# Two pairs of heads taken by turns at the end of an attention stage, and a routing step asked for earlier

## The chip, the cores and the metric

The kernel runs on one core of one Trainium2 chip. The metric is device microseconds of one execution; less is better. Shown times are medians of several runs of the same program. The engines are TensorE (PE in the rows, PEld for its weight loads), VectorE (DVE), ScalarE (ACT), GpSimd (POOL) and SyncE (SP, which here only issues DMAs). Each works through its own list of instructions in the order in which they stand there, and waits at an instruction until what it needs is there.

## The reference, cut to what matters

Three stages in float32, on 2 batches of 8 heads, 768 positions, head size 64:

```python
# 1. attention: a band of |i - j| < 16, and blocks of 32 keys (max of k, mean of v)
scores_l = where(|pos_i - pos_j| < 16, q @ k.T / 8, -1e9)
scores_s = q @ k.reshape(B, H, 24, 32, D).max(3).T / 8 + log(32)
a = softmax(concat([scores_l, scores_s]));  out = a @ concat([v, v_blockmean])
# 2. experts: x [1536, 512]; logits = x @ w_gate; all (token, expert) pairs in falling order of
#    logit, each token to its first expert that holds under 192 tokens so far
out[mask_e] = relu(x[mask_e] @ w1[e]) @ w2[e]          # 8 experts, 192 tokens each
# 3. h = x @ w_in; s = h * softmax(h); layer norm of s times g_ln; out = ln @ w_out
```

## The kernel before, in words

**The units.** The attention runs in 24 units. A unit is (batch, pair of heads, group), where a group is four of the twelve blocks of 64 queries. The list `units` (line 322) numbers them: batch by batch, pair by pair, group by group. A unit passes through three steps: `score` (line 325; four products on PE, L331, then on DVE the mask and the row's extreme, L337, then four exponentials on ACT, L340), `attnT` (L347 turns the weights on PE, L349 empties PSUM on ACT into `aT`) and `pv` (L360 multiplies with the values on PE; DVE makes a reciprocal, L363 and L364, and writes the scaled result into `x`, L367).

**What feeds a pair.** `prep` readies a pair's keys and queries in three steps: GpSimd or DVE copy the keys (L275 `kr`), PE turns keys (L291) and queries (L299) into the PSUM tile `T`, of which there are two, DVE (L293) or ACT (L302) empty it into `kTw` and `qbd`.

**What a group gives.** When all four pairs of a batch are done for a group, its 256 tokens are whole. Then `pv` stores them to HBM (L371), `xT` turns each block of 128 tokens on PE (L381) and empties it on ACT (even blocks, L386) or DVE (odd blocks, L384), and `logits` multiplies by the gate (L393); DVE copies the result into `L` (L395). Batch 1 has blocks 6 to 11, two for each group. `pA` (two in PSUM) serves `attnT` and `xT`, `pO` (two) serves `pv` and `logits`.

**What follows.** The routing of the first expert begins with `head` (line 125): some twelve short DVE instructions over blocks of `L`. It is called twice for the first expert: for blocks 0 to 7 inside the attention (line 450), for blocks 8 to 11 by `route(0)` after it. Only then does `route(0)` go on: a search in five rounds of DVE and PE, the expert's index, its weights' DMA, its products. The whole second half of the kernel hangs on this.

**What sets the order.** A table `plan` gives each step a due time counted in units; the steps are written in rising order of it. For a step of a unit `u`: `score` at u, `attnT` at u + 1.9, `pv` at u + 3.3 (for the last three), `prep` of a pair at the index of its first unit less 4.5, 3.5 and 2.5, `xT` at the index of the last pair's unit + 4.6 and + 5.3, `logits` 1.1 later. PE and SP keep the order in which the steps are written. DVE, ACT and POOL are ordered by a scheduler from its own estimates. Three chunks of the third stage's weights (`raw`, 512 KB each) are also split in this stretch, in six instructions each: L70 and L77 on ACT, L72, L74, L75 and L78 on DVE.

Of the kernel before, what the change touches and what calls it, by code (L numbers as in the profile page):

```python
# [21 lines left out]
def tile_attention_moe_solu(ctx, tc, q, k, v, w_gate, w1, w2, w_in, w_out, g_ln, out):  # L22
    nc = tc.nc
    B, H, S, D = q.shape
# [4 lines left out]
    HP = H // 2  # L29
# [132 lines left out]
    r0 = ctx.enter_context(tc.tile_pool(name="r0", bufs=1))  # L162
    SPLIT = NJ * 2 // 3
    T0 = {}
# [155 lines left out]
            e.tensor_copy(a[:, :NT - 1, 80:WIN], a[:, 1:, 16:32])  # L320

    units = [(b, hp, g) for b in range(B) for hp in range(HP) for g in range(3)]
    ST, AT, XS = {}, {}, {}

    def score(u):
# [74 lines left out]
    def at(u, f, *a):  # L400
        plan.setdefault(u, []).append((f, a))

    for u in range(NU):
        b, hp, g = units[u]
# [42 lines left out]
    with tc.manual_schedule(engines={mybir.EngineType.PE, mybir.EngineType.SP}):  # L447
        for n in range(3):
            prep(0, 0, n)
        at(27.71, head, r0, T0, 0, SPLIT)  # L450
        for u in sorted(plan):
            for f, a in plan[u]:
                f(*a)
# [514 lines left out]
```

## Time and profile before

| | us |
|---|---|
| runs shown (3): median, lowest, highest | 483.68, 482.17, 484.4 |
| profiled execution, its own time | 481.84 |
| its span in the trace | 480.1 |
| PE busy | 444.0 (92%) |
| DVE busy | 273.8 (57%) |
| ACT busy | 175.1 (36%) |

The span is what the trace covers; the run's own time is 1.74 us longer. The last PE instruction of the attention ends at 100.9 us of the span, and the second part of `head` begins at 101.21. Up to there PE, DVE and ACT work on different units side by side, and which of them is late changes from stretch to stretch. From there to about 125 us PE mostly waits for short DVE instructions, one after another; then PE is busy nearly without a break to the end.

### The profile page before, as it was taken

To read this page: it belongs to the slowest core of one execution; us is meant where nothing else is said; L and a number is where in the kernel's file an instruction comes from. 1 tells how busy PE (TensorE), PEld (TensorE's weight loads), DVE (VectorE), ACT (ScalarE), POOL (GpSimd) and SP (SyncE) were. 2 spreads that over 40 slices of the span, in tenths; PEclk is the share of its full clock that TensorE was granted. 3 is DMA by queue.
4 is the path that set the end of the run, shared out by engine and by line. 5 is a ranking of instruction groups with operands and counts; after the bars stand their busy time and mean duration, and the time that the engine had idled before them with its cause. 6 is when DMAs were issued, how large, how long until landed. Compare 5 with 4: busy or idle time off the path is not lost.

```text
span 480.1 us, 9909 instructions
## 1 busy us (share of the span) xinstructions
PE 444.0 (92%) x3809; PEld 385.4 (80%) x3809; DVE 273.8 (57%) x1049; ACT 175.1 (36%) x425; POOL 58.9 (12%) x120
## 2 busy tenths in 40 slices
PE   2899999856989999999999999999999999999994
PEld 1668688735888998788888888888898899998773
DVE  8668576977596879960756249153742404132441
ACT  3678877700243336411313213231131314222331
POOL 8221200001010020020001100201102000101001
PEclk9999999977999999999999999999999999999998
DMA  9969961273889487066019102900752740000001
GB/s 205 219 147 208 231 170 58 89 255 125 271 251 308 122 303 224 2 200 206 1 40 339 50 1 88 319 0 4 248 155 81 224 124 1 23 1 12 11 23 44
DMA packets 92463, 64.62 MB, mean 135 GB/s; under 512 B 25728, under 2 KB 87168, under 8 KB 92416
## 3 DMA queue, kind: packets, MB, share of 16 engines
q1 hardware_dynamic: 88848, 51.93, 39.2%
q0 software_dynamic: 1984, 6.29, 3.7%
q10 hardware_dynamic: 1584, 5.77, 3.5%
q8 instruction: 30, 0.49, 0.4%
q14 instruction: 17, 0.14, 0.1%
HBM read 56.51 MB, written 6.29 MB: 131 GB/s over the span
## 4 chain that ended last, share of the span: by engine, by line
PE 74%; DVE 13%; ACT 4%; DMA 4%; issue 3%; POOL 1%; POOLq 0%; SPq 0%; ACTq 0%; DVEq 0%
PE m L695 30%; PE h L760 13%; PE o L803 11%; PE pS L331 4%; PE pO L360 2%; DVE ge L123 2%; PE pr L501 2%; PE pA L347 2%; PE tr L667 1%; DVE ex L769 1%; PE T L291 1%; PE T L254 1%; PE T L299 1%; DMA kn<-in_k_dram 1%; DVE ch L74 1%
## 5 line engine op out<-in xcount | busy, mean ns | idle before, releaser
L695 PE MATMUL m<-xs,wr 128*128 128x192 f32 x384 | 77.4, 333 | 0.2 <-ACT xs L673 0.2
L695 PEld LDWEIGHTS m<-xs,wr 128*128 128x128 f32 x384 | 63.2, 190 | 4.7 <-PE o L803 0.8
L743 DVE TENSOR_TENSOR yl<-m,yh 128x128 fp32r<-128x128 f32 (+1 forms) x64 | 16.2, 253 | 73.4 <-ACT yh L742 72.7
L712 ACT ACTIVATE hT<-m 128x192 f32<-128x192 f32 x64 | 21.2, 332 | 90.6 <-PE m L695 77.1
L695 PE MATMUL m<-hT,wh 128*128 128x192 f32 x256 | 49.9, 327 | 0.0
L695 PE MATMUL m<-hT,wl 128*128 128x192 f32 x256 | 49.2, 327 | 0.0
L695 PEld LDWEIGHTS m<-hT,wl 128*128 128x128 f32 x256 | 43.3, 189 | 3.2
L695 PEld LDWEIGHTS m<-hT,wh 128*128 128x128 f32 x256 | 43.3, 189 | 3.2
L742 ACT CAST yh<-m 128x128 fp32r<-128x128 f32 (+1 forms) x64 | 15.2, 238 | 82.8 <-PE m L695 73.9
L340 ACT ACTIVATE s<-s,mx 128x120 f32<-128x120 f32 x96 | 31.4, 387 | 11.9 <-DVE mx L337 11.8
L760 PE MATMUL h<-wiH,yh 128*128 128x512 f32 x96 | 34.5, 447 | 0.0
L803 PE MATMUL o<-woH,lh 128*128 128x512 f32 x96 | 30.8, 433 | 1.3 <-ACT lh L792 1.3
L760 PE MATMUL h<-wiH,yl 128*128 128x512 f32 x96 | 32.0, 421 | 0.0
L803 PE MATMUL o<-woL,lh 128*128 128x512 f32 x96 | 31.9, 429 | 0.0
L760 PE MATMUL h<-wiL,yh 128*128 128x512 f32 x96 | 31.8, 419 | 0.0
L331 PE MATMUL pS<-kTw,qbd 128*128 128x120 f32 x192 | 27.3, 287 | 4.6 <-DVE kTw L314 3.6
L331 PEld LDWEIGHTS pS<-kTw,qbd 128*128 128x128 f32 x192 | 24.4, 199 | 6.4 <-issue 4.8
L765 DVE TENSOR_REDUCE st<-h 128x1 f32<-128x1024 f32 x12 | 14.7, 1224 | 26.0 <-PE h L760 25.5
L123 DVE TENSOR_TENSOR ge<-e,ios 128x1536 bf16<-128x1536 bf16 (+3 forms) x37 | 29.0, 783 | 0.8
L803 PE MATMUL o<-woH,ll 128*128 128x512 f32 x96 | 29.3, 417 | 0.0
L337 DVE CUSTOM_DVE_ANT_0 s<-pS,mask 128x120 f32<-128x120 f32 x96 | 21.4, 278 | 12.0 <-PE pA L347 5.2
L501 PEld LDWEIGHTS <-ge 128*128 128x128 bf16 (+1 forms) x420 | 13.8, 96 | 15.2 <-DVE ge L123 10.2
(184 smaller groups left out, 797.7 us busy)
## 6 DMA issues: line engine op xcount, KB each, us to landing
wr<-in_moe_w_dram SPq DMA_DIRECT2D x24, 512.0 KB
wl<-in_moe_w_dram SPq DMA_DIRECT2D x20, 512.0 KB
wh<-in_moe_w_dram SPq DMA_DIRECT2D x20, 512.0 KB
raw<-in_moe_w_out_dram ACTq DMA_DIRECT2D x8, 512.0 KB
Vw<-in_v_dram SPq DMA_DIRECT2D x20, 192.0 KB
kn<-in_k_dram SPq DMA_DIRECT2D x8, 384.0 KB
qn<-in_q_dram SPq DMA_DIRECT2D x8, 384.0 KB
xd<-x SPq DMA_DIRECT2D x6, 512.0 KB
```

The lines of the kernel that those rows point to most:

```text
L123: nc.vector.tensor_tensor(out, x.rearrange("p (j t) -> p j t", t=2)[:, :, None, :].to_broadcast([128, n // 2, b - a, 2]), ios[:, None, a:b ...
L331: nc.tensor.matmul(p[:, n, :], qbd[i][:, t, :], kTw[i][:, t, :], start=True, stop=True)
L337: nc.vector.tensor_tensor_reduce(s[:, n, :], p[:, n, :], m, scale=1.0, scalar=3.0e38, op0=OP.add, op1=OP.min, accum_out=mx[:, n:n + 1])
L340: EXPS[u] = nc.scalar.activation(s[:, n, :], s[:, n, :], AF.Exp, bias=mx[:, n:n + 1], scale=-1.0)
L501: nc.tensor.matmul(pr[0:nb, 0:E], ge[:, j // 2, :nb, j % 2], oh[:, j, :], start=j == 0, stop=j == NJ - 1)
L695: nc.tensor.matmul(p[:, :CAP], w[:, d, o:o + 128], rhs[:, d], start=d == 0, stop=d == n - 1)
L712: after(ph, "h", f, nc.scalar.activation(h[:, f], p[:, :CAP], AF.Relu))
L742: a = nc.scalar.copy(hi, s[:, s0:s0 + n])
L743: nc.vector.tensor_tensor(YL[k][:, d, c:c + n], s[:, s0:s0 + n], hi.bitcast(F32), op=OP.subtract)
L760: nc.tensor.matmul(ps, a[:, d, :], w[:, d, 512 * s:512 * s + 512], start=n == 0, stop=n == len(mm) - 1)
L765: nc.vector.tensor_reduce(st[:, 0:1], p, axis=AX.X, op=OP.max)
L803: nc.tensor.matmul(p, a[:, f, :], w[:, f, :], start=n == 0, stop=n == len(mm) - 1)
```

## The change

```diff
     units = [(b, hp, g) for b in range(B) for hp in range(HP) for g in range(3)]
+
+    units[-6:] = [(B - 1, hp, g) for g in range(3) for hp in (HP - 2, HP - 1)]
     ST, AT, XS = {}, {}, {}
...
         for n in range(3):
             prep(0, 0, n)
-        at(27.71, head, r0, T0, 0, SPLIT)
+        at(26.1, head, r0, T0, 0, SPLIT)
```

The last six units were (1,2,0) (1,2,1) (1,2,2) (1,3,0) (1,3,1) (1,3,2); now they are (1,2,0) (1,3,0) (1,2,1) (1,3,1) (1,2,2) (1,3,2). So unit 19 completes group 0 (before: unit 21), unit 21 completes group 1 (before: 22), unit 23 still completes group 2. All due times that are taken from a unit's index move: `prep` of pair (1,3) by two units (14.5, 15.5, 16.5 in place of 16.5, 17.5, 18.5), `xT` and `logits` of blocks 6 and 7 by two, of blocks 8 and 9 by one. The first part of `head` is due at 26.1 in place of 27.71. No instruction is added or taken away. SP and POOL have the same rows in the same order in both kernels, and from the second part of `head` on so have PE, DVE and ACT. In the changed kernel every line after 322 has a number greater by 2.

**PE where pair (1,3) is prepared.** Before, from the `pv` behind the score of unit 14 on (`T<-..kr` are keys, `T<-..qn` queries, `kTw_142` belongs to units 15 to 17):

```order
L360 MATMUL pO<-Vw,aT 64x65 x8
L291 MATMUL T<-ident,kr 128x128 x2
L299 MATMUL T<-ident,qn 128x128 x3
L331 MATMUL pS<-kTw_142,qbd_143 128x120 x4
L381 MATMUL pA<-ident,x 128x128 x4
L347 MATMUL pA<-ident,s 120x128 x4
L360 MATMUL pO<-Vw,aT 64x65 x8
L299 MATMUL T<-ident,qn 128x128 x3
L381 MATMUL pA<-ident,x 128x128 x4
```

And the same place in the changed kernel:

```order
L362 MATMUL pO<-Vw,aT 64x65 x8
L291 MATMUL T<-ident,kr 128x128 x2
L299 MATMUL T<-ident,qn 128x128 x3
L291 MATMUL T<-ident,kr 128x128 x4
L333 MATMUL pS<-kTw_142,qbd_143 128x120 x4
L383 MATMUL pA<-ident,x 128x128 x4
L349 MATMUL pA<-ident,s 120x128 x4
L362 MATMUL pO<-Vw,aT 64x65 x8
L299 MATMUL T<-ident,qn 128x128 x3
L291 MATMUL T<-ident,kr 128x128 x2
L299 MATMUL T<-ident,qn 128x128 x3
L383 MATMUL pA<-ident,x 128x128 x4
```

The four key transposes of pair (1,3) now stand directly behind two other fillings of `T`, ahead of the score of unit 15, and in the next unit three fillings of `T` stand in a row.

**PE at the end of the attention.** Before, from the score of unit 23 on (`pA<-ident,s` is `attnT`, `pA<-ident,x` is `xT`, `pO<-wg,xT` is `logits`):

```order
L331 MATMUL pS<-kTw_136,qbd_137 128x120 x4
L360 MATMUL pO<-Vw,aT 64x65 x8
L347 MATMUL pA<-ident,s 120x128 x4
L360 MATMUL pO<-Vw,aT 64x65 x8
L347 MATMUL pA<-ident,s 120x128 x4
L360 MATMUL pO<-Vw,aT 64x65 x8
L381 MATMUL pA<-ident,x 128x128 x4
L360 MATMUL pO<-Vw,aT 64x65 x8
L381 MATMUL pA<-ident,x 128x128 x8
L393 MATMUL pO<-wg,xT 32x8 x16
```

And in the changed kernel, from the `pv` behind the score of unit 23 on:

```order
L362 MATMUL pO<-Vw,aT 64x65 x8
L383 MATMUL pA<-ident,x 128x128 x4
L349 MATMUL pA<-ident,s 120x128 x4
L362 MATMUL pO<-Vw,aT 64x65 x8
L383 MATMUL pA<-ident,x 128x128 x4
L395 MATMUL pO<-wg,xT 32x8 x16
L349 MATMUL pA<-ident,s 120x128 x4
L362 MATMUL pO<-Vw,aT 64x65 x8
L395 MATMUL pO<-wg,xT 32x8 x16
L383 MATMUL pA<-ident,x 128x128 x4
L362 MATMUL pO<-Vw,aT 64x65 x8
L383 MATMUL pA<-ident,x 128x128 x4
```

`xT` of block 6 moved ahead of `attnT` of unit 22, and before the last `pv` (unit 23) there now stand three `xT` and two `logits` in place of one `xT`. Behind the last row shown come, in the changed kernel, the logits of blocks 8 and 9, then `xT` of blocks 10 and 11 together, then their logits.

**ACT at the end of the attention.** Before, behind the copy of `aT` of unit 21 (`cy` and `wiH` belong to the split of the weights' chunks):

```order
L77 CAST wiH<-ch 128x512
L340 ACTIVATE s<-s,mx 128x120 x2
L349 COPY aT<-pA 120x512
L340 ACTIVATE s<-s,mx 128x120 x2
L77 CAST wiH<-ch 128x512
L70 ACTIVATE cy<-raw 128x512
L349 COPY aT<-pA 120x512
L386 COPY xT<-pA 128x512
```

And in the changed kernel:

```order
L77 CAST wiH<-ch 128x512
L342 ACTIVATE s<-s,mx 128x120 x4
L77 CAST wiH<-ch 128x512
L70 ACTIVATE cy<-raw 128x512
L388 COPY xT<-pA 128x512
L351 COPY aT<-pA 120x512 x2
```

The copy of `aT` of unit 22 stood between the exponentials of unit 23, ahead of the third chunk's `cy`; now it stands behind that `cy` and behind the copy of `xT` of block 6.

## Rows read from the trace of the kernel before

**Rows 1.** The page's line of busy time by engine.
```profile
PE 444.0 (92%) x3809; PEld 385.4 (80%) x3809; DVE 273.8 (57%) x1049; ACT 175.1 (36%) x425; POOL 58.9 (12%) x120
```

**Rows 2.** Busy time by stretch: PE, PEld, DVE, ACT, POOL; then clock, DMA, GB/s.
```profile
60.00:88.00 28.00, 28.00 (x495) 24.71 (x493) 21.83 (x118) 22.56 (x60) 2.08 (x6) 1.00 0.33 99
88.00:94.00 6.00, 4.02 (x62) 3.06 (x60) 5.92 (x25) 4.21 (x10) 0.00 (x0) 1.00 0.27 87
94.00:100.00 6.00, 5.37 (x197) 4.39 (x196) 5.47 (x23) 2.27 (x4) 0.00 (x0) 1.00 0.72 262
101.00:102.00 1.00, 0.34 (x8) 0.24 (x7) 0.90 (x9) 0.00 (x0) 0.00 (x0) 0.55 0.07 16
```

**Rows 3.** Timeline, last `pv` to second part of `head`: start, length, engine, line, operation.
```profile
94.04 0.73 PE L360 MATMUL pO<-Vw,aT 120*64 120x65 f32 x16
...
94.71 1.09 PE L381 MATMUL pA<-ident,x 128*128 128x128 f32 x8
94.81 0.16 DVE L363 TENSOR_SCALAR r<-pO 128x4 f32<-128x4 f32 x1
...
96.01 0.41 DVE L367 TENSOR_TENSOR x<-pO,r 128x256 f32<-128x256 f32 x1
...
98.05 0.22 DVE L137 TENSOR_REDUCE v<-L 128x8 f32<-128x64 f32 x1
...
99.16 0.69 DVE L384 COPY xT<-pA 128x512 f32<-128x512 f32 x1
99.77 0.16 DVE L395 COPY L<-pO 128x8 f32<-128x8 f32 x1
...
100.21 0.21 DVE L123 TENSOR_TENSOR ge<-e,ios 128x128 bf16<-128x128 bf16 x1
...
100.50 0.42 PE L393 MATMUL pO<-wg,xT 128*32 128x8 f32 x27 [0.20 <-issue]
...
100.97 0.17 DVE L395 COPY L<-pO 128x8 f32<-128x8 f32 x1 [0.55 <-PE pO L393]
...
101.21 0.18 DVE L137 TENSOR_REDUCE v<-L 128x4 f32<-128x32 f32 x1
```

**Rows 4.** The chain that ended last, 84 to 103 us: start, length, what.
```profile
96.45 4.77 DMA xd<-x
```

**Rows 5.** Timeline, units 13 to 15.
```profile
57.42 0.96 POOL L275 COPY kr<-kn 128x384 f32<-128x384 f32 x2 [1.74 <-DMA kn<-in_k_dram]
...
61.58 0.49 PE L299 MATMUL T<-ident,qn 128*128 128x128 f32 x3
61.78 0.42 DVE L293 COPY kTw<-T 128x256 f32<-128x256 f32 x1
61.91 1.05 PE L331 MATMUL pS<-kTw,qbd 128*128 128x120 f32 x8
...
63.77 0.73 PE L360 MATMUL pO<-Vw,aT 120*64 120x65 f32 x16
...
64.95 0.42 DVE L367 TENSOR_TENSOR x<-pO,r 128x256 f32<-128x256 f32 x1
```

**Rows 6.** Timeline behind the score of unit 23.
```profile
88.06 0.73 PE L360 MATMUL pO<-Vw,aT 120*64 120x65 f32 x16
...
89.41 0.59 ACT L349 COPY aT<-pA 120x512 f32<-120x512 f32 x1
...
89.96 0.41 DVE L367 TENSOR_TENSOR x<-pO,r 128x256 f32<-128x256 f32 x1
...
90.89 0.17 DVE L364 RECIPROCAL r<-r 128x4 f32<-128x4 f32 x1
...
91.51 0.69 ACT L70 ACTIVATE cy<-raw 128x512 f32<-128x512 f32 x1 [0.43 <-DMA raw<-in_moe_w_in_dram]
```

**Rows 7.** The instructions on tile `qn`: ns least, median, most; first and last start.
```profile
L299 PE MATMUL T<-ident,qn x42: 272/273/330, 16.7 to 77.3; 128*128 128x128 f32 x42
...
L299 PE MATMUL pA<-ident,qn x6: 421/421/421, 7.7 to 8.8; 128*128 128x128 f32 x6
```

## The prediction

> **What bounds the kernel now.** I read the page's busy times first: PE is busy for 444.0 of 480.1 us [rows 1]. That is an average, so the table of busy time by stretch comes next, for the stretch that the change touches. From 60 to 88 us PE is busy for all of 28.00 us: there PE is the bound, and what makes it wait is lost. From 88 to 94 it drops to 4.02 of 6 while DVE has 5.92, and from 94 to 100 DVE still has 5.47 of 6 [rows 2]: the end of the attention belongs to DVE. Then I read the timeline up to the second part of `head`, at 101.21 [rows 3]. Everything later hangs on that instruction, and none of its order changes, so the forecast is one question: how far does 101.21 move? The chain of waits names a store of `x`, 4.77 us from 96.45, as the last thing before it [rows 4]. I don't follow it there: `head` reads `L`, not that store, and DVE ran up to 101.14 on a copy that PE's logits released (100.97 + 0.17) [rows 3].
>
> **The middle: `prep` of pair (1,3), two units earlier.** PE's list now has five fillings of `T` within two units where three stood, and `T` has two buffers.
>
> *First wait.* The key transposes of (1,3) follow three query transposes, which begin at 61.58 and are done when the score begins, 61.91. They need a buffer that DVE empties with L293, 61.78 + 0.42 = 62.20 [rows 5]. PE waits 0.29, with the score of unit 15 queued behind.
>
> *Second wait.* In the next unit, queries, keys and queries stand in a row, and the last filling needs DVE to have emptied the keys. Counted from the start of the `pv` at 63.77, DVE ends that unit's multiplication at 64.95 + 0.42 = 65.37 and would do L293 next, to 65.79: 2.02 later. PE has work of its own for 0.73 (`pv`), 0.33 (three transposes) and 0.22 (two more, at 0.11 each): 1.28 [rows 5]. It waits about 0.7. Exponentials and masks of the same units shift with it.
>
> Together 1.0. The transposes themselves are no cost, since they only stand elsewhere. Bounds: nothing, if the time comes back before 88 us (PE's full 28.00 speak against that: there is no idle time to give back), and 2.0, if nothing of PE's own work covers the second wait. I take 1.0.
>
> Free edits: the copy of the keys on GpSimd, done at 57.42 + 0.96 = 58.38, is first needed at 61.91, 3.5 us later [rows 5], and its load keeps its place on SP; if that cover were gone, the wait would appear on PE ahead of the key transposes. The earlier due time of `head`'s first part only places it among other DVE work, and its results have no reader until the search. Stores of groups 0 and 1 go out earlier, into DMA queues with little to do.
>
> **The tail.** I work in the times of before and add the middle at the end.
>
> *PE waits where it did not.* `xT` of block 6 now stands ahead of `attnT` of unit 22. PE ends the `pv` at 88.06 + 0.73 = 88.79; `xT` needs unit 19's multiplication, 89.96 + 0.41 = 90.37 [rows 6]. PE waits 1.6, with `attnT` behind it.
>
> *ACT passes it on.* The copy of `aT` of unit 22 ran at 89.41. Now it stands behind L70, which waits for its chunk and ends at 91.51 + 0.69 = 92.20 [rows 6], and behind the copy of block 6. With 0.59 each, block 6 is out at 92.8 and `aT` at 93.4, where it was out at 90.00: 3.4 later.
>
> *DVE, then, is late.* `xT` of block 7 waits for block 6's buffer, 92.8, and takes half of 1.09 [rows 3] and a short way to DVE: its copy starts at about 93.45. From there DVE has, in its order, to the first part of `head`: that copy, three chunk instructions, two multiplications, six short ones. A copy takes 99.77 - 99.16 = 0.61 [rows 3]; a multiplication and a chunk instruction together 90.89 - 89.96 = 0.93 [rows 6], so 0.61 and 0.32; the short ones 0.1 to 0.2. 4 x 0.61 + 2 x 0.32 + 6 x 0.13 = 3.9, so `head` starts at 97.35 (98.05 before [rows 3]).
>
> *The last `pv`* needs a buffer of `pO` that this train's last copy of logits frees: 97.35, where it began at 94.04, and it ends at 98.08. DVE meanwhile does `head`'s first eight instructions, 99.16 - 98.05 = 1.11 [rows 3], to 98.45. Then come six short ones at 0.1 (five from 99.77 to 100.21 take 0.44 [rows 3]), mixed from `head` and the reciprocal, and the last multiplication: 98.45 + 0.6 + 0.41 = 99.45, where it ended at 96.01 + 0.41 = 96.42 [rows 3]. 3.0 later.
>
> *From there to `head`'s second part* there were 101.21 - 96.42 = 4.79. Now less stands in it, since blocks 6 to 8 are done: a copy of block 9, 0.69; its logits, 0.42; eight transposes, 1.09; a copy, 0.69; logits, 0.42; the copy into `L`, 0.17 [rows 3]. Sum 3.5, so 102.95: 1.75 later than 101.21.
>
> Sum: 1.0 + 1.75 = 2.75. The profiled execution took 481.84, so 484.6; the median of the runs shown lies 1.84 above it, so 486.4 on that scale, rounded to 486.5. If both middle waits vanish it is 485.4, with 2.0 in the middle 487.5. Own range 485.3 to 487.6.
>
> **The rivals.**
>
> *Faster: the turns empty the tail.* With blocks 6 to 9 done early, the last `pv` could start at 94.04 as before. It ends at 94.77; reciprocal and multiplication (0.16, some 0.25, 0.41) end at 95.6; eight transposes, copy, logits and the copy into `L` (1.09, 0.69, 0.42, 0.17 [rows 3]) at 98.05: 3.1 earlier, less 1.0 in the middle gives 2.1 less, 481.6. This decides where the last `pv` does not wait for the DVE train. For it: PE has 2 us of idle time from 88 to 94 [rows 2]. Against it: the copy of `aT` behind L70. 8 in 100.
>
> The Trainium skill, "Perfetto Trace Analysis", section "Optimization Strategy", says that interleaving regimes with different contended engines may help; by it the tail would come out as in this rival. The rows bear it out only in part, as DVE is full on both sides of the seam, 5.92 and 5.47 of 6 [rows 2].
>
> *No change: DVE's work alone sets the tail.* No instruction is added, and DVE idles only 0.08 of 88 to 94 and 0.53 of 94 to 100 [rows 2]. If it stays as full in the new order, 101.21 moves by 0 to 0.6 less, and the middle's 1.0 is left, or is made up by DVE-bound work later: 483.1 to 484.7. Against it: DVE must wait for block 7's copy and, at the end, for PE's last transposes. 25 in 100.
>
> *Slower: the last store gates the second part.* If the chain [rows 4] is right after all, 4.77 stay between the last multiplication and `head`: 99.45 + 4.79 = 104.24, 3.0 later, with the middle 4.0: 487.7. 7 in 100.
>
> *Slower: PE's clock falls before the last transposes.* In 101 to 102, when PE had begun to wait, the granted clock was 0.55 [rows 2], so half of the stretch or more at 1.2 in place of 2.4 GHz; transposes early in the kernel took 421 ns against 273 [rows 7]. Last `pv`, transposes and logits, 0.73 + 1.09 + 0.42 + 0.42 = 2.7, would grow by 0.35 to 0.7 of that: 0.9 to 1.9, 487.4 to 488.4. It decides if PE's waits grow long behind the score of unit 23. Against it: in 88 to 94 PE idled 2 of 6 and the clock stayed 1.00 [rows 2]. 10 in 100.
>
> The Trainium skill, "Perfetto Trace Analysis", section "Matmul Optimizations", says that the matmul engine scales its power with utilization, so that matmuls should run back to back; by that the price of this rival would be due. The row of 88 to 94 does not bear it out for gaps such as these.
>
> **How the numbers follow.** 0.5% of 483.68, which is about what a measurement here can tell from no change, is 2.4: slower begins at 486.1, faster ends at 481.3. My forecast has 50 in 100, 32 of them above 486.1; with the two slow rivals that makes 0.49 for slower. The no-change rival and the lower part of the forecast give 0.45 for same, with a little of the fast rival, whose larger part lies near 481.3: 0.06 for faster. The range reaches down to 483.0, which takes in the no-change rival, and up to 488.8, a little over the clock's; the fast rival is left out.
>
> **What would show it.** In the new trace: PE idle ahead of the key transposes of (1,3) at 62, and again near 66 ahead of the query transposes; every score after that about 1 later. PE idle for 1.6 ahead of `xT` of block 6; the copy of `aT` of unit 22 behind L70; the last `pv` near 98.4 instead of 94.04, and the first part of `head` ahead of its multiplication; the second part near 104, and from there to the end 480.1 - 101.2 = 378.9 as before. I am wrong if PE runs through at 62 and 66, if `aT` of unit 22 leaves ahead of the chunk's wait, or if the last `pv` comes by 96.

## The result and the profile after

| | before | changed |
|---|---|---|
| median of the runs, us | 483.39 (482.17 to 485.04, 8 runs) | 488.05 (485.21 to 489.36, 8 runs) |
| profiled execution, us | 481.84 | 487.64 |
| its span, us | 480.1 | 485.9 |

The ratio is 1.0087, 95% interval 1.0071 to 1.0102: slower by 3.4 to 4.9 us, 4.2 in the middle, by all runs on both sides (the two medians alone lie 4.7 apart). A second measurement of the changed kernel gave 1.0094 (1.0075 to 1.0112). The forecast was 486.5 with a range of 483.0 to 488.8.

The page's line of busy time hardly moves, as no work was added [rows 1]:

```profile
PE 447.1 (92%) x3809; PEld 388.3 (80%) x3809; DVE 274.5 (56%) x1049; ACT 175.1 (36%) x425; POOL 58.9 (12%) x120
```

Busy time by stretch (PE, PEld, DVE, ACT, POOL, then clock, DMA share, GB/s) shows the two places. PE, which had no gap from 60 to 88 us, now has 1.70 of idle time there, and DVE is no longer full from 94 to 100, where it had 5.47 of 6 [rows 2]: it waits too.

```profile
60.00:88.00 28.00, 26.30 (x466) 22.77 (x465) 19.66 (x104) 20.14 (x54) 2.08 (x6) 1.00 0.34 99
88.00:94.00 6.00, 4.84 (x62) 4.18 (x60) 5.98 (x29) 5.65 (x16) 0.00 (x0) 1.00 0.27 91
94.00:100.00 6.00, 4.29 (x111) 3.15 (x109) 4.95 (x16) 2.83 (x5) 0.00 (x0) 1.00 0.27 101
```

A warning on absolute times. The score of unit 14, the last one ahead of any moved instruction on PE, begins at 59.23 in the profiled execution of before, at 59.96 in that of the changed kernel, and between 59.68 and 61.32 in the other kernels below. So this first part differs from execution to execution, and I compare stretches that begin behind it: from the score of unit 14 to the last score (the middle), from there to `head`'s second part (the tail), and from there to the end of the span (the rest).

| kernel | score 14 | last score | `head` 2 | middle | tail | rest | ratio to before (95%) |
|---|---|---|---|---|---|---|---|
| before | 59.23 | 87.08 | 101.21 | 27.85 | 14.13 | 378.9 | 1 |
| changed | 59.96 | 90.14 | 106.06 | 30.18 | 15.92 | 379.8 | 1.0087 (1.0071, 1.0102) |
| changed again | 60.73 | 90.91 | 106.63 | 30.18 | 15.72 | 379.6 | 1.0094 (1.0075, 1.0112) |
| order only | 59.82 | 89.99 | 105.98 | 30.17 | 15.99 | 380.7 | 1.0064 (1.0040, 1.0087) |
| prep alone | 59.73 | 89.64 | 103.85 | 29.91 | 14.21 | 378.6 | 1.0053 (1.0033, 1.0073) |
| xT old | 59.92 | 90.36 | 104.51 | 30.44 | 14.15 | 379.1 | 1.0026 (1.0009, 1.0043) |
| both old | 59.95 | 87.66 | 101.89 | 27.71 | 14.23 | 379.7 | 0.9998 (0.9981, 1.0015) |
| prep one later | 59.68 | 87.39 | 106.14 | 27.71 | 18.75 | 379.7 | 1.0041 (1.0022, 1.0059) |
| the same again | 60.46 | 88.17 | 105.88 | 27.71 | 17.71 | 381.6 | one run |
| keys early only | 59.99 | 88.22 | 104.70 | 28.23 | 16.48 | 380.0 | 1.0083 (1.0052, 1.0115) |
| last queries later | 60.30 | 89.66 | 106.60 | 29.36 | 16.94 | 379.9 | 1.0105 (1.0084, 1.0127) |
| xT 6 behind | 59.96 | 89.59 | 104.12 | 29.63 | 14.53 | 379.3 | 1.0066 (1.0045, 1.0087) |
| chunk early | 59.96 | 89.40 | 104.28 | 29.44 | 14.88 | 380.3 | 1.0048 (1.0026, 1.0070) |
| combined | 61.32 | 89.02 | 104.57 | 27.70 | 15.55 | 378.9 | 1.0004 (0.9990, 1.0018) |

The stretches come from one profiled execution each, the ratios from several runs. The changed kernel has +2.33 in the middle and +1.79 in the tail, 4.12 together, which is what the ratio says. The two profiled executions differ by 5.8 in their spans: 0.73 more stands ahead of the score of unit 14, where the order is the same, and 0.95 in the rest, which has no order by kernel.

**The middle.** The timeline of PE from unit 14 to the score of unit 18, with one line of ACT (start, length, engine, line, operation, in brackets the idle time and what ended it) shows four waits:

```profile
62.31 0.49 PE L299 MATMUL T<-ident,qn 128*128 128x128 f32 x3
63.09 0.63 PE L291 MATMUL T<-ident,kr 128*128 128x128 f32 x4 [0.28 <-DVE kTw L293]
63.55 1.05 PE L333 MATMUL pS<-kTw,qbd 128*128 128x120 f32 x8
...
66.45 0.38 PE L291 MATMUL T<-ident,kr 128*128 128x128 f32 x2
67.40 0.55 PE L299 MATMUL T<-ident,qn 128*128 128x128 f32 x3 [0.56 <-DVE kTw L293]
...
75.08 0.74 PE L362 MATMUL pO<-Vw,aT 120*64 120x65 f32 x16
75.51 0.59 ACT L388 COPY xT<-pA 128x512 f32<-128x512 f32 x1
76.15 0.66 PE L383 MATMUL pA<-ident,x 128*128 128x128 f32 x4 [0.34 <-ACT xT L388]
76.74 0.23 PE L395 MATMUL pO<-wg,xT 128*32 128x8 f32 x3
77.49 0.43 PE L395 MATMUL pO<-wg,xT 128*32 128x8 f32 x29 [0.52 <-issue]
77.85 0.37 PE L333 MATMUL pS<-kTw,qbd 128*128 128x120 f32 x1
```

The first two were forecast at these places with this releaser, DVE's copy out of `T`. The third was not: `xT` waits for a buffer of `pA` that ACT has not yet emptied. The fourth stands inside a block of logits, and the profile names nothing that it waited for; the last section comes back to it.

**The tail.** From the timeline of all engines, around L70 and on to `head`'s second part:

```profile
93.49 0.33 PE L383 MATMUL pA<-ident,x 128*128 128x128 f32 x1 [1.16 <-DVE x L369]
...
94.60 0.66 ACT L70 ACTIVATE cy<-raw 128x512 f32<-128x512 f32 x1 [0.92 <-DMA raw<-in_moe_w_in_dram]
...
95.17 0.57 ACT L388 COPY xT<-pA 128x512 f32<-128x512 f32 x1
...
95.63 0.59 ACT L351 COPY aT<-pA 120x512 f32<-120x512 f32 x1
...
95.79 0.66 PE L383 MATMUL pA<-ident,x 128*128 128x128 f32 x4 [0.87 <-ACT xT L388]
...
96.48 0.69 DVE L386 COPY xT<-pA 128x512 f32<-128x512 f32 x1 [0.69 <-PE pA L383]
...
100.33 0.22 DVE L137 TENSOR_REDUCE v<-L 128x8 f32<-128x64 f32 x1
...
100.37 0.71 PE L362 MATMUL pO<-Vw,aT 120*64 120x65 f32 x16 [0.44 <-DVE L L397]
...
101.98 0.42 DVE L369 TENSOR_TENSOR x<-pO,r 128x256 f32<-128x256 f32 x1
...
106.06 0.18 DVE L137 TENSOR_REDUCE v<-L 128x4 f32<-128x32 f32 x1
```

This is the forecast's sequence: `xT` of block 6 waits for a multiplication, ACT stands at L70 until the chunk is there, the copy of block 6 and `aT` of unit 22 come behind it, DVE gets block 7 only then, and the last `pv` waits for the copy of logits at the end of DVE's train. The chain that ended last (start, length, what) says the same. In before it led through the third chunk as well, but from L70 on to DVE's own work:

```profile
91.51 0.70 ACT cy L70
...
92.23 0.26 DVE ch L72
```

Now `xT` of block 6 is its next link:

```profile
90.56 3.96 DMA raw<-in_moe_w_in_dram
...
94.60 0.66 ACT cy L70
95.27 0.48 ACT xT L388
...
95.79 0.67 PE pA L383 x4
```

### The profile page after: what moved, and what is told of

It reads as the page before. It is cut to its first block, busy times and chain, and to the rows that moved or that the text cites. A ratio compares the mean times of both kernels' runs of the same rounds, so it can differ in the third digit from the quotient of the medians.

```text
span 485.9 us, 9907 instructions
## 1 busy us (share of the span) xinstructions
PE 447.1 (92%) x3809; PEld 388.3 (80%) x3809; DVE 274.5 (56%) x1049; ACT 175.1 (36%) x425; POOL 58.9 (12%) x120
## 4 chain that ended last, share of the span: by engine, by line
PE 73%; DVE 14%; ACT 5%; issue 4%; DMA 3%; POOL 1%; POOLq 0%; SPq 0%; DVEq 0%; ACTq 0%
PE m L697 30%; PE h L762 13%; PE o L805 11%; PE pS L333 4%; PE pO L362 2%; PE pr L503 2%; DVE ge L123 2%; PE pA L349 1%; PE tr L669 1%; DVE ex L771 1%; ACT s L342 1%; PE T L254 1%; DVE ch L74 1%; DMA kn<-in_k_dram 1%; PE o L833 1%
```

## The experiments

Kernels are edits of the changed one unless said otherwise. The theory in all of them: `prep` of (1,3) makes the middle late, `xT` of blocks 6 to 9 the tail, and they add.

**Order only.** `head`'s first part as before:

```diff
-        at(26.1, head, r0, T0, 0, SPLIT)
+        at(27.71, head, r0, T0, 0, SPLIT)
```

> The new order of units, with the first part of head due at 27.71 as in the kernel before. Theory (two delays, one in the middle from prep of pair (1,3), one in the tail from xT of blocks 6 to 9): the due time of head carries nothing, so 488.1 +- 0.7, that is 4 to 5 more than before, with the last score near 90 and the second part of head near 106. Rival A (head's first part, asked for earlier, pushes into the DVE train ahead of the last multiplication and makes the tail late): 1 to 2 less than the changed kernel, 486 to 487.

Measured: 486.49, ratio 1.0064; middle 30.17, tail 15.99. The median is rival A's figure, not the one expected. But the stretches are those of the changed kernel, and so is the order: PE, ACT and GpSimd have the same instructions in the same order in both traces, DVE too but for two short neighbours behind the last `pv` that change places. So the due time of `head` carries nothing, rival A falls, and 486.49 (484.7 to 488.5) beside 488.05 (485.2 to 489.4) shows how far two medians of one order can lie apart. The profiled execution is one of the longer runs, 488.44.

**Prep one later.**

```diff
-                at(max(u0 + g - 4.5, g + 2.9), prep, *divmod(i, HP), g)
+                at(max(u0 + g - (4.5 - 1 if i == B * HP - 1 else 4.5), g + 2.9), prep, *divmod(i, HP), g)
```

> The changed kernel with prep of pair (1,3) one unit later (15.5, 16.5, 17.5 in place of 14.5, 15.5, 16.5). Theory: the crowding of T goes and with it the middle's delay; PE has no wait ahead of the key and query transposes of (1,3) and the last score comes 1.0 (my forecast of the middle) to 2.3 (what the trace shows, 3.06 less the 0.73 already there before the first moved instruction) earlier: 485.7 to 487.1. Rival B (the middle's delay comes from the turns themselves, the masks, exponentials and copies of two pairs side by side): within 0.5 of the changed kernel, 488. Rival C (the 4.2 is the run's own: the start and the clock in the search): within 0.5 of the changed kernel too.

Measured: 484.98, ratio 1.0041, below the 485.7 to 487.1 expected, and the middle is 27.71, 2.47 shorter than in the changed kernel and 0.14 shorter than before. Rivals B and C fall. The four waits are gone. The timeline of PE at the place of the third shows why it is gone too: three query transposes stand between the `pv` and the `xT`, which follows them without a wait.

```profile
73.14 0.73 PE L362 MATMUL pO<-Vw,aT 120*64 120x65 f32 x16
73.81 0.55 PE L299 MATMUL T<-ident,qn 128*128 128x128 f32 x3
74.19 0.60 PE L383 MATMUL pA<-ident,x 128*128 128x128 f32 x4
74.72 0.44 PE L395 MATMUL pO<-wg,xT 128*32 128x8 f32 x32
75.09 1.15 PE L333 MATMUL pS<-kTw,qbd 128*128 128x120 f32 x8
```

The tail, 18.75, is longer than any other; the profiled run, 487.52, is the longest of the kernel's twelve. The table by stretch shows a granted clock of 0.60 from 94 to 100 and 0.50, the lower of its two levels (1.2 of 2.4 GHz), from 100 to 104, after a stretch in which PE was busy for only 3.56 of 6:

```profile
88.00:94.00 6.00, 3.56 (x48) 2.69 (x47) 4.77 (x21) 4.52 (x11) 0.00 (x0) 1.00 0.50 175
94.00:100.00 6.00, 5.43 (x108) 4.54 (x108) 4.90 (x21) 1.79 (x3) 0.00 (x0) 0.60 0.24 90
100.00:104.00 4.00, 3.21 (x74) 2.79 (x73) 1.81 (x10) 0.33 (x1) 0.00 (x0) 0.50 0.33 126
```

**Prep one later, again**, the same kernel in one run:

> The kernel with prep of (1,3) one unit later once more, for one look: its profiled execution had a granted clock of 0.50 from 96 us on and 18.75 from the last score to head's second part. Theory (that clock is the execution's own): in an execution whose clock stays at 1.00 to there, 15.9 as in the changed kernel, and 484 to 485.5. Rival (the kernel itself makes the clock fall there): 18.7 again, and 487.

Measured: one run, 489.19; middle 27.71 again, tail 17.71, and again a low clock, 0.51 from 94 to 100:

```profile
94.00:100.00 6.00, 5.63 (x97) 4.46 (x99) 4.39 (x16) 2.03 (x5) 0.00 (x0) 0.51 0.21 78
```

So the expectation that it was a single execution's matter failed. It is not always there either: 9 of the 12 timed runs of this kernel lie between 483.6 and 486.0, three between 487.0 and 487.6.

**xT old.** `xT` and logits of batch 1 at the due times of before, with `head` at 27.71:

```diff
-                u = units.index((b, HP - 1, g)) + (4 if b else 5.4)
+                u = (NU - 3 + g if b else units.index((b, HP - 1, g))) + (4 if b else 5.4)
...
-        at(26.1, head, r0, T0, 0, SPLIT)
+        at(27.71, head, r0, T0, 0, SPLIT)
```

> The changed kernel with xT and logits of blocks 6 to 11 at the due times they have in the kernel before, and so the first part of head at 27.71 too; prep of (1,3) stays early. Theory: the tail's part goes (copy of aT of unit 22 ahead of the chunk's wait again, last pv 3 earlier), the middle's stays: the stretch from the last score to the second part of head is 14.1 as before instead of 15.9; 1.8 less than the changed kernel, 486.3. Rival D (the tail is late because the units' weights come in another order, not because of xT): within 0.5 of the changed kernel, 488. Rival C: 488.

Measured: 484.97, ratio 1.0026; tail 14.15, as before to 0.02, middle still 30.44. `head`'s second part in DVE's timeline:

```profile
104.51 0.19 DVE L137 TENSOR_REDUCE v<-L 128x4 f32<-128x32 f32 x1
```

The tail's part is shown to come from `xT`; rival D falls. The ratio is a little lower than a middle of +2.6 would ask (1.0054). Prep alone, below, has the same lines in the same order on PE, DVE, ACT and GpSimd (only the units' data differ) and gave 1.0053, so the order is not what makes the difference; the two intervals overlap.

**Both old.** The two edits together, so that of the change only the order of the units is left, and a `prep` of (1,3) that is still one unit earlier than before (15.5 in place of 16.5):

```diff
-                at(max(u0 + g - 4.5, g + 2.9), prep, *divmod(i, HP), g)
+                at(max(u0 + g - (4.5 - 1 if i == B * HP - 1 else 4.5), g + 2.9), prep, *divmod(i, HP), g)
...
-                u = units.index((b, HP - 1, g)) + (4 if b else 5.4)
+                u = (NU - 3 + g if b else units.index((b, HP - 1, g))) + (4 if b else 5.4)
...
-        at(26.1, head, r0, T0, 0, SPLIT)
+        at(27.71, head, r0, T0, 0, SPLIT)
```

> The new order of units with prep of (1,3) one unit later and with xT, logits and head's first part at the due times of the kernel before: only the order of the units is left of the change. Theory: both delays go, so as before within 0.7, 482.9 to 484.2; second part of head near 101. Rivals B and D: 2 or more above before, 485.5 or more. Rival C: 488.

Measured: 483.27, ratio 0.9998 (0.9981 to 1.0015). Middle 27.71, tail 14.23. The last score is 0.58 and `head`'s second part 0.68 behind before, and the score of unit 14 was already 0.72 behind (timeline of PE, then DVE):

```profile
87.66 0.60 PE L333 MATMUL pS<-kTw,qbd 128*128 128x120 f32 x4
...
101.89 0.19 DVE L137 TENSOR_REDUCE v<-L 128x4 f32<-128x32 f32 x1
```

The turns by themselves cost nothing and bring nothing that the interval, 0.7 to 0.9 us to either side, would show.

**Prep alone**, on the kernel before, with its order of units:

```diff
-                at(max(u0 + g - 4.5, g + 2.9), prep, *divmod(i, HP), g)
+                at(max(u0 + g - (4.5 + 2 if i == B * HP - 1 else 4.5), g + 2.9), prep, *divmod(i, HP), g)
```

> The kernel before, its order of units, with prep of pair (1,3) alone moved two units earlier (14.5, 15.5, 16.5). Theory: the middle's delay comes without the turns, last score 2.3 later than before as counted from unit 13, with the same four places on PE: 0.28 ahead of the key transposes, 0.56 ahead of the query transposes, then about 0.34 for ACT's copy of xT and 0.5 inside the logits; tail as before (14.1 from the last score to head's second part): 483.4 + 2.3 = 485.7. Rival (turns and prep together are needed): within 0.5 of before.

Measured: 485.44, ratio 1.0053; middle 29.91 (+2.06), tail 14.21. The same four places in PE's timeline, the fourth shorter:

```profile
62.86 0.63 PE L291 MATMUL T<-ident,kr 128*128 128x128 f32 x4 [0.28 <-DVE kTw L293]
67.17 0.55 PE L299 MATMUL T<-ident,qn 128*128 128x128 f32 x3 [0.56 <-DVE kTw L293]
75.92 0.66 PE L381 MATMUL pA<-ident,x 128*128 128x128 f32 x4 [0.33 <-ACT xT L386]
76.99 0.43 PE L393 MATMUL pO<-wg,xT 128*32 128x8 f32 x29 [0.25 <-issue]
```

Early `prep` alone makes the middle late, without the turns.

**Keys early only.** Second and third step of `prep` one unit later, the first stays early:

```diff
-                at(max(u0 + g - 4.5, g + 2.9), prep, *divmod(i, HP), g)
+                at(max(u0 + g - 4.5 + ((0, 1, 1)[g] if i == B * HP - 1 else 0), g + 2.9), prep, *divmod(i, HP), g)
```

> The changed kernel with the second and third step of prep of (1,3) one unit later: only the first four key transposes stay early. Mended theory: only the wait at 63 is left, 0.45 by starts of the instructions, last score 28.2 to 28.4 behind the score of unit 14. Rival (T stays crowded through the next unit): a second wait near 67, 28.9.

Measured: middle 28.23, as expected, with a single wait left on PE:

```profile
63.12 0.63 PE L291 MATMUL T<-ident,kr 128*128 128x128 f32 x4 [0.28 <-DVE kTw L293]
```

The time, 486.33, is no measure of the middle: the profiled run, 486.36, has a tail of 16.48 with a clock of 0.61 from 100 to 104.

**Last queries later.** Only the third step one unit later:

```diff
-                at(max(u0 + g - 4.5, g + 2.9), prep, *divmod(i, HP), g)
+                at(max(u0 + g - 4.5 + ((0, 0, 1)[g] if i == B * HP - 1 else 0), g + 2.9), prep, *divmod(i, HP), g)
```

> The changed kernel with only the third step of prep of (1,3) (three query transposes) one unit later, so that on PE they stand again between a pv and an xT near 76. Theory, as mended by the runs so far (two waits for T, and a third near 76 where the moved query transposes no longer cover ACT's copy of xT): the waits of 0.28 and 0.56 at 63 and 67 stay, the third (0.34 on xT) is gone; last score 28.9 to 29.0 behind the score of unit 14 in place of 30.2 in the changed kernel and 27.85 in the kernel before. Rival (the third wait follows from the delay of the first two, whatever stands ahead of the xT): the third wait stays, 29.4 or more.

Measured: middle 29.36, which is close to the rival's figure. The wait near 76 is gone, but PE's timeline has one of the same size at 72, on the `xT` from which the query transposes were taken away:

```profile
67.74 0.55 PE L299 MATMUL T<-ident,qn 128*128 128x128 f32 x3 [0.56 <-DVE kTw L293]
72.00 0.66 PE L383 MATMUL pA<-ident,x 128*128 128x128 f32 x4 [0.34 <-ACT xT L388]
```

My expectation forgot that the transposes had been a cover where they stood. That speaks for the cover as the reason, though not by the number I gave, and against the rival: with the first two waits as before, there is no wait where the cover stands. Time: 488.18, ratio 1.0105, with a clock of 0.72 from 94 to 100.

**xT 6 behind.** 0.4 later for blocks 6 and 7, so that `attnT` of unit 22 goes first:

```diff
-                u = units.index((b, HP - 1, g)) + (4 if b else 5.4)
+                u = units.index((b, HP - 1, g)) + ((4 + 0.4, 4, 4)[g] if b else 5.4)
```

> The changed kernel with xT and logits of blocks 6 and 7 due 0.4 later, so that on PE xT of block 6 stands behind attnT of unit 22 (and the steps behind it move by one place); head's first part stays at 26.1 and prep of (1,3) stays early. Theory (the tail is late because aT of unit 22 waits behind the third chunk's L70 on ACT): the copy of aT leaves ACT ahead of L70 again, and the second part of head comes about 1.2 of the 1.8 earlier: from the last score 14.7 in place of 15.9; 486.9 where the changed kernel has 488.1. Rival (the last pv waits for the copy of logits into L whatever is ahead of it): 15.9 stays, 488.

Measured: tail 14.53, 1.39 of the 1.79 gone. On ACT the copy of `aT` of unit 22 leaves ahead of L70 again:

```profile
91.93 0.58 ACT L351 COPY aT<-pA 120x512 f32<-120x512 f32 x1
...
93.72 0.69 ACT L70 ACTIVATE cy<-raw 128x512 f32<-128x512 f32 x1
```

One place in PE's order (the steps behind it move along) carries most of the tail's delay. The time, 486.71, is near the 486.9 expected, but in part by luck: the traced execution, 485.07, is one of the two shortest of six, and its two stretches are only 2.2 longer than before's, as the fourth wait of the middle is missing too (29.63).

**Chunk early.** A third buffer for raw chunks, `aT` with one less:

```diff
-        at((15, 16, 21.5)[i], load_in, cva, i, 2)
+        at((15, 16, 21.5)[i], load_in, cva, i, 3)
...
-        a = wk.tile([KEYS, 4, 128], F32, name="aT", bufs=6)
+        a = wk.tile([KEYS, 4, 128], F32, name="aT", bufs=5)
```

> The changed kernel with three buffers for the raw chunks in place of two, so that the third chunk's load need not wait until DVE is through with the first chunk, and aT with five buffers in place of six to make room. PE has the same order. Theory: L70 finds its chunk and does not wait the 0.92 of the changed kernel; block 6's copy, aT of unit 22 and all behind come about 0.9 earlier, second part of head 15.0 behind the last score in place of 15.9; about 487.2. Rival (DVE's train alone decides, L70's wait is hidden): 15.9, 488.

Measured: L70 does not wait for a DMA and runs at 92.27, 2.87 behind the last score in place of 4.46; the tail is 14.88, 1.04 shorter. So the chunk's wait is on the path, with 1.04 where 0.9 was expected. ACT's timeline:

```profile
92.27 0.65 ACT L70 ACTIVATE cy<-raw 128x512 f32<-128x512 f32 x1
```

The time is 485.36; more than the tail is gone because the fourth wait of the middle is missing too (29.44).

**Combined**, the try at a better kernel: `prep` of (1,3) one unit later and:

```diff
-                u = units.index((b, HP - 1, g)) + (4 if b else 5.4)
+                u = units.index((b, HP - 1, g)) + ([5.7, 4.7, 3.7][g] if b else 5.4)
...
-        at(26.1, head, r0, T0, 0, SPLIT)
+        at(27.75, head, r0, T0, 0, SPLIT)
```

> The turns with prep of (1,3) one unit later than in the changed kernel, xT of the three groups at 5.7, 4.7 and 3.7 units behind the unit that completes them, head's first part at 27.75. A try at a better kernel. Theory: no delay in the middle, last score as before; xT of block 6 behind attnT of unit 22, so the tail is no longer than before and 0.3 to 0.6 shorter at best: 482.8 to 483.3, not to be told from before. Rival (turns cost something of their own): 484 to 485.

Measured: 483.87, ratio 1.0004 (0.9990 to 1.0018): no better than before. The middle is 27.70. The tail of the profiled execution, 15.55, is longer than before's, against the expectation; its run, 485.25, is the longest of twelve. It has an idle time inside the last logits, again without a releaser, where before has 0.20 [rows 3]:

```profile
103.68 0.60 PE L395 MATMUL pO<-wg,xT 128*32 128x8 f32 x28 [1.18 <-issue]
```

**The changed kernel again,** with no edit:

> The changed kernel once more, beside the kernel before on the same chip: 487 to 488, ratio 1.006 to 1.010 by what was measured; last score 29.4 to 30.2 behind the score of unit 14, 15.9 from there to head's second part.

Measured: 487.66, ratio 1.0094; middle 30.18, tail 15.72.

## Why the prediction was right, and where it was off

*The direction and the two places* are shown by both old (neither, 0.9998), xT old and prep alone (only the middle) and prep one later (middle gone): two separate delays that add. They are shown by the stretches; the times of the kernels between the two ends spread too much to show them.

*The tail, forecast at 1.75, is 1.79.* Less the 3.06 by which the last score is later, the changed trace gives: L70 ready at 91.54 (91.51 forecast), DVE's copy of block 7 at 93.42 (93.45), first part of `head` at 97.27 (97.35), the last `pv` at 97.31 (97.35), the last multiplication's end at 99.34 (99.45), `head`'s second part at 103.00 (102.95). The mechanism is shown by xT 6 behind and chunk early. The working could be this close because each step was an instruction of DVE or ACT with a duration from before and a queue that the order shows.

*The middle, forecast at 1.0, is 2.33: this is the step that failed, by its size.* The two waits on `T` were 0.28 and 0.56 where I had 0.29 and 0.7. By the starts of the instructions they cost 0.45 (63.09 - 62.31, less the 0.33 that three transposes take [rows 5]) and 0.68 (67.40 - 66.45, less the 0.27 that two transposes take in before, 72.81 to 73.08 below), 1.13 together: that term was right. What I left out are the third and fourth places, 0.40 (76.15 - 75.08, less the 0.67 from a `pv` to the next instruction, 73.14 to 73.81 above) and 0.74 (77.85 - 76.74, less 0.37, 74.72 to 75.09 above). All four make 2.27 of 2.33. The sentence that failed is "the transposes themselves are no cost, since they only stand elsewhere": in their old place, two key and three query transposes stood between that `pv` and that `xT` and gave ACT time to empty `pA`. PE's timeline in before, with no wait at this place:

```profile
72.14 0.73 PE L360 MATMUL pO<-Vw,aT 120*64 120x65 f32 x16
72.81 0.44 PE L291 MATMUL T<-ident,kr 128*128 128x128 f32 x2
73.08 0.49 PE L299 MATMUL T<-ident,qn 128*128 128x128 f32 x3
73.41 0.60 PE L381 MATMUL pA<-ident,x 128*128 128x128 f32 x4
```

I asked what hides the moved work, not what the moved work hides. That they were the cover is borne out by prep one later and by last queries later, where the wait went to the place they had been taken from; no run takes the cover away without the first two waits. The fourth wait is of another kind (last section): it goes with early `prep` (0.52 or 0.53 in the changed kernel, order only and changed again, 0.78 in xT old, 0.25 in prep alone), but is missing in xT 6 behind, chunk early, keys early only and last queries later. The forecast had no term for it. The middle passed my upper bound, 2.0, by the fourth wait: where only the first three are there it is 1.59 (chunk early) and 1.78 (xT 6 behind). So 488.05 lies above the forecast's own range (485.3 to 487.6). That the wider range holds it is luck: the clock's rival had stretched it to 488.8, and the clock stayed at 1.00 in both profiles of the changed kernel. The prediction also counts five fillings of `T` in the two units where there are six; no sum hangs on it.

*Rival, faster: the turns empty the tail.* It did not come: the last `pv` waited for DVE's train. In both old, where no delay is left, the turns bring 0.9998. So the rule of interleaving (the Trainium skill, "Perfetto Trace Analysis", section "Optimization Strategy") finds nothing to gain in the orders that were run, as [rows 2] suggested with DVE full on both sides.

*Rival, DVE's work alone sets the tail.* Falls: DVE idled 1.05 of 94 to 100 while it waited for block 7 and others.

*Rival, the last store gates `head`.* Falls: from the end of the last multiplication, 101.98 + 0.42 = 102.40, to `head`'s second part there are 3.66 in the changed trace, less than the 4.77 of the store [rows 4]; and the last store has landed at 105.17, 0.89 ahead of `head`'s second part.

*Rival, the clock falls before the last transposes.* It does, in some executions. With the changed order of the tail, in xT 6 behind with one step of it moved, nine profiled executions stand above (changed, changed again, order only, the two of prep one later, keys early only, last queries later, xT 6 behind, chunk early); five of them had a granted clock under 0.75 in some stretch between 94 and 104, and their tails are 15.99 to 18.75, the others' 14.53 to 15.92. With the tail of before (before, xT old, both old, prep alone) none fell before `head`'s second part, but for 0.95 in the last 1.2 us of before. In order only it fell (0.72 from 94 to 100), in the two of the changed kernel it did not, with nearly the same order, so the order alone does not decide it. I had put the price at 0.9 to 1.9, and the runs don't separate it: the fall in order only left a tail of 15.99 beside 15.92, and of the 2.83 by which the tail of prep one later is longer than the changed kernel's, 0.41 was there at L70, which waited longer for its chunk, ahead of the fall. It shows in single instructions: the last eight transposes took 1.97 there against 1.09 in the changed trace. In the changed kernel's own two profiles the clock stayed at 1.00 to there, so it is not needed for the 4.2, but the spread of its runs (485.2 to 489.4) leaves room for it. The Trainium skill, "Perfetto Trace Analysis", section "Matmul Optimizations", asks for back-to-back matmuls because the engine scales its power with utilization. The traces agree in part: the clock fell behind PE's 3.56 of 6 in prep one later, and stayed at 1.00 behind 4.29 of 6 in the changed kernel (94 to 100). That 88 to 94 bore no fall in before, which I held against this rival, was one execution of another order.

## What to carry to other kernels

When a step is moved, ask three things of it: what it waits for in its new place (the buffers it now shares), who waits behind it there, and what it had covered in its old place. A new order of work units that changes due times of eleven other steps is several changes: the order itself was worth nothing, and two of the steps that it carried along were worth all of the 4 us. Compare traces by stretches between events that both have, since the time ahead of the first moved instruction may differ by 2 us between executions.

## What the runs showed that was not expected

The first 60 us differ by up to 2.09 us between executions that run the same PE instructions (score of unit 14 at 59.23 to 61.32). In the trace of the changed kernel this begins at 15.4 us, where eight products take 1.90 in place of 1.20. The rest of the kernel behind `head`'s second part differs as well, from 378.6 to 381.6, with no order by kernel.

And PE has idle times of 0.2 to 1.2 us within blocks of logits that no semaphore event in the profile ends, the fourth wait of the middle among them. Between the score of unit 14 and `head`'s second part there are nine of them in the fourteen traces. A reading of the kept traces suggests what they wait for: PE's own instructions. The page lists a DMA queue for instructions with 30 packets of 16 KB:

```profile
q8 instruction: 30, 0.49, 0.4%
```

PE's records (3809 matmuls, 3809 weight loads and some hundred others) come to some 258 for each packet. The nine idle times stand at just two places in PE's list, 1022 to 1024 records apart, which is about four packets. All nine end 1.2 to 1.5 us after a packet of this queue has landed, the fifth for the place in the middle, the ninth for the one in the last logits. In the changed kernel the fifth lands at 76.20 and PE goes on at 77.49. In before it lands at 70.57, and PE comes to that place 3.4 us later, without a wait. Wherever there is no idle time at the two places, at least 1.2 us have passed since the landing. This fits all fourteen traces, but no run moves the packet alone, and why it comes later with early `prep` stays open.
